# The first channel product of the last batch: 15 products for 3x3 by 3x2 blocks in place of 11 of 12

## The chip, the cores and the metric

One core of a Trainium2 chip runs the whole program. The time is device microseconds of that core. The kernel before took 606.97 us, the median of three runs (605.12 to 607.92). Its profiled execution took 605.11 us, of which the profile's span covers 603.4 us.

## What is computed

A delta-rule recurrence (linear attention), followed by a mixer with a low-rank part and two channel products. Cut to what matters:

```python
# attention, batch 4, 8 heads, 768 tokens, 48 per head -> x of (4, 768, 384)
for t in range(S):
    y[:, :, t] = einsum('bhd,bhde->bhe', q[:, :, t], state)
    v_old = einsum('bhde,bhd->bhe', state, kt)
    state = state + bt * einsum('bhd,bhe->bhde', kt, vt - v_old)
# mixer, for every batch
h = xt @ U @ V                           # rank 32, over the tokens
u = x + h.transpose(0, 2, 1)             # (768, 384)
ch = maximum(u @ w_ch1, 0.0) @ w_ch2     # 384 -> 1536 -> 384
out = u + ch
```

The change concerns `u @ w_ch1` (and the cut at zero behind it) for the last of the four batches. There `w_ch1` is 3 blocks of 128 input channels by 12 blocks of 128 hidden channels (`f` is a hidden block), and `u`, turned so that channels lie on partitions, is 3 blocks of 128 channels by 768 tokens.

## The kernel before, in words

**Stages.** For each batch, `recur` runs the recurrence in 12 chunks of 64 tokens, with `norms`, `grams` and `blocks` preparing each half batch. `load_weights` (L742) reads the weights as 64-bit numbers and converts them in the first 120 us or so. The mixer of a batch goes in three groups of 256 tokens: `front(b, i)` adds the low-rank part (the adds are L1073) and turns the result (L1090, copied by L1093); `wide(b, i)` makes the first channel product (`channels`, L1142 and L204), the sums for the second (`add_up`, L1163, and `last_sum`, L1170) and the second product (`narrow`, L1230) as seven half-products of 128 by 192 in place of eight, whose results `gather` adds to X (L1176) and stores. The mixer of one batch overlaps the recurrence of the next.

**The last batch** has no recurrence to overlap. All its 768 tokens are turned into `ut_last` first, and its first channel product runs for all tokens at once in `quick(f)` (L848), for the six pairs of hidden blocks f and f+6. Such a pair is 2 x 3 blocks of weights by 3 x 2 blocks of tokens (two halves of 384 tokens), which would be 12 products of 128x128 by 384 columns. Two of the three channel blocks are handled by a scheme of seven products in place of eight (Strassen's, in Winograd's form), the third by four plain ones: 11 in all. It needs sums of weight blocks (`weight_sums`, L823: n1, s2, s4 for each f, and one in place, L836) and mixes of token blocks (`token_sums`, L839, five, L845). All products are issued by `mm` at L859. Running sums in PSUM are copied out by ACT (L877, L881, L886), added to by DVE (L868) and cut at zero by ACT (L863, or L927 straight from PSUM). The output `hs_last` lies in `slot0`, the turned tokens in `slot1`; both are free once the recurrence is over.

**PSUM.** Eight banks: four pairs, and two 'mix' banks (6 and 7) that overlap the last pair. A quick part takes a pair (px, pz) and one mix bank (py).

**The order of work** is written out in full: ORDER (L52) is a list of tokens, one for each step of one of some 660 parts. A part is a generator, numbered in the sequence in which parts are begun; its yields are steps on a named engine, or needs that must have been emitted before. `.2` on a token says which bank pair or mix bank the step takes, `q` that it goes in quarters of the array. Each engine works its steps in the order of this list; the semaphores between engines follow from the data.

Of the kernel before, what the change touches and what calls it, by code (L numbers as in the profile page):

```python
# [23 lines left out]
def kernel(ctx: ExitStack, tc: tile.TileContext, q: bass.AP, k: bass.AP, v: bass.AP, beta: bass.AP, moe_U: bass.AP, moe_V: bass.AP, moe_w_ch1: bass.AP, moe_w_ch2: bass.AP, out: bass.AP):  # L24
# [28 lines left out]
    1 0 1 0 1 0 1 0 37 1 21 22 21 22 21 2 14.0 21 22 36 22 176 38 2 176 15.1 39 36 39 38 178 177.2 37 36 178  # L53
    20 36 179.3 38 177 39 177 38 177 43 17.0 179 39 179 179 18.1 26 19 179 37 23 181 2 24 23 2.3 179 2 37 23
    182.1 2 123 2 12 2 179 32.3 24 12 180 26 182 183 24 184.0 19 24 177 12 19 43 177 29.3 184 177 19 186 19
    182 187.2 19 19 33.3 19 188 41 40 184 30.1 187 40 19 3.3 187 124 187 3 19 187 124 19 40 187 19 190 124 19
    191.0 3 23 3 122 19 192 124 187 19 122 191 19 19 191 191 122 191 19 125 191 191 196 196.2 35 194 197 194.1
    197 34 198 41 196 197 41 194 196 41 198 127 189.3 3 197 12 194 40 197 27 125 198 185.0 27 198 127 198 198
    194.2 27 122 189 199 122 197 122 194 34 126 196.1 42 194 34 196 34 25 194 34 126 194 25 34 193 194.2 185
    194 193 34 193 34 193 34 194 122 194.2 194 196 193 196 193 196 194 122 194 196.1 196 27 200 195 122 196  # L60
    195 5.2 122 128 195 34 42 195 185 5.1 128 201 195 122 34 196.0 5 34 196 189 195 5 34 196 4.2 34 196 34
    202.3 34 6.1 202 4 202 34 34 6.0 4.2 6 204 122 6 207.3 208 204.1 4 129 208 206 208 206.0 129 208 122 208
    4.2 122 209 204 209 4 210 206 122 208 206 4.2 209 207 122 209 211.0 209 122 204 207 4 209 4.1 212 204.2 4
    204 122 207 206.1 204 130 204 206 204 130 122 203 4.3 122 213 214.2 211 206 206 211 206 204.1 203 4 122
    211 4.3 203 204 4 131 203 206.0 205 203 131 206 203 205 4.3 204 122 206 204.1 122 205 216 4 122 205 204
    214 205 132 206.0 214 205 206 132 204 52 215.3 204 206 4.1 122 206 4 122 217 218.0 4.1 215 122 214 215
    141.2 215 4 133 133 218 141 122 137 4.1 122 218 7.2 54 218 4 219 54 7.0 53 122 54 142 7 142 53 7 142 53
    142 142 122 134 142 122 134 143 142 53 143 220 143 53 4.1 221.2 4 8.0 122 4.1 143 4 135 143 135 143 54 144
    143 144 54 56 144 122 53 144 122 8.1 53 54 144 8 144 54 222 145 145 145 122 8 145 144 136 4.0 221 4 223.1
    136 221 4.0 46 221 56 145 4 54 122 145 53 122 224 146 4.2 223 4 225.0 223 122 4.2 223 146 145 4 49.1 226  # L70
    146 227 226 4.2 225 4 229.1 225 226 4.2 225 146 4 146 226 4.0 229 4 230.2 229 122 4.0 229 146 4 231 122
    232.1 4.0 146 230 4 232 122 230 230 46.0 232 66 233 47.2 234 66 233 147 232 66 235 236.0 233 66 233 237.1
    236 66 67 236 152.2 66 67 237 236 236 237 66 67 237 51 237 67 152 67 50.0 67 147 55 152 44 67 147 238 69
    44 147 67 147 69 66 148.1 147 44 55 148 51 69 152.2 147 55 148 69 51 239.0 55 152 56 148.1 239 59 55 239
    51 56 62.2 148 51 51 149.0 247 51 63.2 51 149 249 148 68 149 250 68 59.2 51 148 68 51 150.0 253 68 51 252
    60.1 68 51 151.2 255 150 55 150 257 68 153.1 151 258 68 256.0 151 259 55 240 260 254.2 55 240 256 153 68
    243 254 254 254 240 254 51 153.1 241 228.2 241 153 241 243 261 51 51 51 51 244 51 265 265.1 65 256 265 262
    228 265 242 265.1 265 267 244 228 256 263 256 265 265 265 267.2 64 264 267 264 265.1 264 245 267 268 57
    264 44 154.0 57 265 265 245 269 264 57 264 154 57 154.2 270 265.1 265 64 270 265 267.0 267 154 64 246 267
    265 267 267 64 266 64 266 271 267.2 266 64 271 9.0 266 272q 64 9 64 272 64 9.1 272 283.0 272 64 283 283 9  # L80
    272 64 9.0 284 285.1 64 267 267 273 9 266 64 64 273 64 274 286 64 64 274 64 266 275 287 288 64 275 64 276
    289 64 288 276 64 64 277 290 288 64 277 64 64 279 291 64 64 292 279 292 64 64 292 64 9.2 248.0 293 9 294
    9.2 280 9 248 248 64 278 267.2 267 64 9.0 267 295 285 9 267 280 285 64 285 281 299 78 301 298 297 298 302
    296.0 298 299.2 298 301.1 299 301 300 298 281 300 299 301 300 300 282 303 303 300 300 298 304 301.2 301
    304 299.1 299 301 305q 301 299 9.2 305 9 9.2 305 299 305 9 9.2 305 9 316.1 317 9.2 296 9 306q 296 296 306
    9.2 306 9 306 9.0 306 9 318.2 319 316 9.0 307q 9 316 316 9.0 307 9 320.1 307 9.0 307 9 9.0 9 307 9.0 321
    320 9 318 320 322 9.0 318 322 79 308 320 9 318 79 322 79 308 79 79 80 324 9.1 251.0 79 80 9 323.2 79 80
    251 9.1 309 251 80 9 82 9.0 82 325.1 9 323 72 9.0 323 79 323 309 9 80 80 72.2 326 80 310 327 82 80 9.0
    328.2 82 9 9.0 328 325 9 325 328 9.0 325 328 310 9 328 73.1 330 331 75.0 332 331 333 329.2 331 334.1 9.0
    334 312q 9 334 334 9.0 77 334 329 312 329 329 336.1 312 312 9 70 70 9.2 312 9 70 77 9.0 76.2 9 77 339 81  # L90
    9.0 337 336 338 9 81 341.2 336 311 9.0 336 313q 9 77 77 77 9.1 313 9 77 342.0 77 313 9.1 313 9 77 9.1 77
    313 9 77 344 342 343 341 340.1 77 341 92 342 77 342 314 92 341 340 92 340 92 77 314 92 93 77 92 93 77 92
    93 77 155.0 93 345 93 77 93 93 335.2 155 346 93 155.1 77 346 92 81 77 315 95 155 85 81 335 81 95 155.0 335
    95 77 85.1 155 81 88.2 347 348 77 347 89.0 360 77 86.1 94 362 77 94 361.2 364 77 94 349q 361 77 94 349 361
    94 156.0 77 349 94 349 77 81 156 366.1 94 77 349 81 367 361 156.0 77 94 366 77 350 361 77 366 156 77 350
    366 77 366 351 368 370 91 351 372 369 90 371 352 369 373 371 352 70 83 371 353 375 83 371 369 374 353 369
    83 374 90 354 376 83 354 90 374 377 365.2 90 90 370.0 372.1 378 372 370 365 371 372 356 370 371 365 95 90
    90 378 356 378 90 379 369 90 372.1 370.0 380 369 372 370 90 372 357 370 90 372 90 370 90 357 381 90 382
    10.2 90 363.1 10 10.0 157.2 10 355 10.0 358 10 90 363 90 358 385 90 363 359 90 386 157 386 10.0 387 384.1
    138 10 157q.2 138 90 10.0 157 388 90 90 388 10 138 138 138 399 10.2 90 383.0 384 383 389q 10 383 138 138  # L100
    384 90 10.2 384 389 10 400.0 138 389 10.1 90 389 10 138 389 90 10.2 401 138 400 10 390q 400 138 90 400
    10.1 390 90 10 402.2 390 10.0 390 10 138 90 10.1 390 10 404 90 403.0 402 405 10.1 402 90 391 402 405 10
    138 90 391 90 90 392 406 405 392 408 104 407 10.2 138 407 393 10 411 410 138 409 138 138 407 412.1 138
    10.2 409 403 10 393 409 403 409 395 413 407 414 403 414 415 10.2 414 408.0 10 408 408 10.2 412 10 410.0
    412 410 106 408.2 412 408 410 106 395 408 408 106 106 106 105 396 394 106 105 416 407 105 106 105 396 417
    105 106 105 397 418 105 105 407 397 419 98 409 101.1 420 409 102.0 421 98.2 422 107 99.1 424 107 107 426
    10.0 427.2 10 420 10.1 107 427 428.0 107 387 427 427 108 398 428 107 10 428 427 428 107 103 428 107 410.1
    429.2 10.0 10 96 410 430 96 10.0 410 430 431q 108 410 10 108 431 96 103 442.1 108 431 10.0 431 10 103 10.0
    103 10 429 103 431 429 103 10.0 429 442 443 10 444.2 103 10.0 103 10 432 442 103 442 103 10.0 423.1 10 103
    10.0 444 103 432 444 10 444 423 423 433 446 103 103 10.0 445.2 103 10 425.1 10.0 425 433 425 10 103 447  # L110
    10.1 445 10 434q 445 448 445 103 10.0 434 10 103 449.1 434 10.2 434 10 448 450.0 10.2 434 10 449 451 103
    10.2 449 103 435 449 10 103 450 103 435 450 119 450 103 119 448 436 452 119 103 119 96 436 119 118 119 121
    103 453 158.1 119 118 103 118 103 118 454 118 438q 103 103 119 438 158 118 454 118 158.2 454 438 103 118
    438 158 438 103 103 158q.0 456 111 455 103 114.1 158 103 115.2 457 111.0 462 120 112.1 120 464 437 439 121
    466 461 117 120 459 460 121 460 120 458 468 120 159.2 460 120 467.0 458 159 120 469.1 467 120 467 439 469
    467 460 469 469 467 116 469 440 458 470 109 458 109 440 471 109 116 441 472 116 472 116 116 116 159q.2 116
# [1197 lines left out]
```

## Time and profile before

| | before |
|---|---|
| median of three runs | 606.97 us (605.12 to 607.92) |
| the profiled execution | 605.11 us, span 603.4 us |
| PE busy | 560.4 us, 93% |
| DVE busy | 391.5 us, 65% |
| ACT busy | 244.1 us, 40% |
| mean granted TensorE clock | 0.955 |
| the rewritten stage (L859) | 515.2 to 557.7 us, 66 products |

PE is matrix products, DVE and ACT the two vector engines that read PSUM and make the sums. A product of fp32 operands leaves two records (two passes), so 66 products are 132 records. "Granted clock" is the share of full speed that TensorE was given. A group's line gives the source line, engine, operation, what is written and read, shapes and count, then busy time and mean duration in ns, then the engine's idle time just before those instructions and what ended it.

### The profile page before, as it was taken

The numbers are of one execution on the slowest core, as the hardware profiler recorded it, in microseconds if no ns is written. First come the engines' busy times: TensorE is split into PE (matmuls) and PEld (weight loads), VectorE is DVE, ScalarE is ACT, GpSimd is POOL, SyncE is SP. The second block draws the span as 40 slices with busy tenths as digits, with TensorE's granted clock in tenths as the row PEclk, the third lists the DMA queues.
The fourth block names the chain that finished last, engine by engine and source line by source line (L and its number), as shares of the span: only waits on it lengthen the run. The fifth ranks groups of instructions, "written<-read, shape, count | busy, mean of one in ns | idle before, by whom it ended". The sixth has DMA issues, their size and how long they took to land. (4 is left out here: it accounts for less than half of the span.)

```text
span 603.4 us, 24671 instructions
## 1 busy us (share of the span) xinstructions
PE 560.4 (93%) x11133; PEld 471.2 (78%) x11133; DVE 391.5 (65%) x979; ACT 244.1 (40%) x520; POOL 98.0 (16%) x169
## 2 busy tenths in 40 slices
PE   5566799999999999999999999999999999999997
PEld 4465778678788788789879877989889769656997
DVE  4899755899896229999983699898413226132542
ACT  2776974652314444263243532622532231344000
POOL 8420140630101032321004203210010000000000
PEclk9957569998999999999999999999999999999999
DMA  9963487730000061520004405200000000000000
GB/s 140 169 165 90 126 204 187 118 74 3 30 0 17 17 101 42 112 52 7 16 3 80 101 5 86 64 20 4 29 2 3 30 2 1 27 1 0 27 27 26
DMA packets 63850, 33.34 MB, mean 55 GB/s; under 512 B 50817, under 2 KB 61825, under 8 KB 63745
## 3 DMA queue, kind: packets, MB, share of 16 engines
q1 hardware_dynamic: 56800, 23.21, 17.6%
q0 software_dynamic: 5344, 8.27, 6.8%
q8 instruction: 87, 1.43, 1.0%
q10 hardware_dynamic: 1600, 0.30, 0.3%
q14 instruction: 19, 0.15, 0.1%
HBM read 27.03 MB, written 4.72 MB: 53 GB/s over the span
## 5 line engine op out<-in xcount | busy, mean ns | idle before, releaser
L1142 PE MATMUL P<-ut,w_sb 128*128 128x256 f32 x384 | 88.7, 384 | 0.3 <-ACT hs L1112 0.2
L1142 PEld LDWEIGHTS P<-ut,w_sb 128*128 128x128 f32 x384 | 71.1, 190 | 11.9 <-issue 1.8
L1230 PE MATMUL P<-w_sb,hs 128*128 128x192 f32 x456 | 79.5, 329 | 0.2 <-DVE X L1176 0.2
L1230 PEld LDWEIGHTS P<-w_sb,hs 128*128 128x128 f32 x456 | 73.9, 190 | 2.0 <-DVE X L1176 0.6
L463 DVE TENSOR_TENSOR xt<-xt,prod 128x112 f32<-128x112 f32 (+21 forms) x200 | 64.6, 323 | 6.9
L462 DVE TENSOR_TENSOR prod<-gs,xt 128x112 f32<-128x112 f32 (+21 forms) x200 | 63.7, 318 | 3.7
L1176 DVE TENSOR_TENSOR X<-X,P 128x192 f32<-128x192 f32 x85 | 29.4, 349 | 49.2 <-PE P L1230 45.8
L1112 ACT ACTIVATE hs<-P 128x512 f32<-128x512 f32 x48 | 28.7, 597 | 72.0 <-PE P L1142 53.7
L204 PE MATMUL P<-ut,w_sb 64*64 64x256 f32 x768 | 52.6, 384 | 1.7 <-ACT hs L1112 1.1
L1230 PE MATMUL P<-w_sb,S 128*128 128x192 f32 x240 | 43.3, 337 | 0.7 <-DVE X L1176 0.7
L1230 PEld LDWEIGHTS P<-w_sb,S 128*128 128x128 f32 x240 | 40.3, 195 | 1.6 <-DVE X L1176 1.4
L714 DVE TENSOR_TENSOR s<-s,P 128x192 f32<-128x192 f32 x40 | 14.0, 350 | 41.9 <-PE P L708 34.4
L304 POOL DMA_DIRECT2D slot<-in_k_dram x44 | 29.4, 674 | 64.5 <-PE P L708 46.9
L605 ACT COPY X<-P 64x192 f32<-64x192 f32 x96 | 30.0, 312 | 21.3 <-PE P L622 19.8
L581 ACT COPY slot<-zz 32x384 f32<-32x384 f32 x64 | 32.5, 509 | 6.9 <-DVE zz L467 3.5
L401 PE MATMUL P<-slot 48*64 48x64 f32 x1536 | 30.8, 232 | 4.6 <-ACT slot L389 4.4
L401 PEld LDWEIGHTS P<-slot 48*64 48x64 f32 x1536 | 28.0, 146 | 8.6 <-ACT slot L389 5.7
L585 POOL MEMSET slot<- 32x384 f32 x32 | 13.3, 421 | 129.7 <-PE P L556 113.5
L378 PE MATMUL P<-ident,slot 128*128 128x128 f32 x192 | 27.2, 294 | 6.8 <-DMA slot<-in_k_dram 6.8
L859 PE MATMUL P<-slot,w_sb 128*128 128x384 f32 x96 | 32.9, 486 | 0.0
L204 PEld LDWEIGHTS P<-ut,w_sb 64*64 64x64 f32 x768 | 25.1, 133 | 9.2 <-ACT hs L1112 1.8
L1230 PE MATMUL P<-w_sb,slot 128*128 128x192 f32 x180 | 30.4, 327 | 0.9 <-DVE X L1176 0.9
(176 smaller groups left out, 993.5 us busy)
## 6 DMA issues: line engine op xcount, KB each, us to landing
X<-in_moe_w_ch_dram SPq DMA_DIRECT2D x12, 384.0 KB, 4.4
out_dram<-X SPq DMA_DIRECT2D x22, 192.0 KB, 1.9
wide<-in_moe_w_ch_dram SPq DMA_DIRECT2D x10, 384.0 KB, 4.3
slot<-in_k_dram SPq DMA_DIRECT2D x48, 72.0 KB, 4.3
slot<-in_k_dram POOLq DMA_DIRECT2D x44, 72.0 KB, 4.5
slot<-in_q_dram POOLq DMA_DIRECT2D x32, 72.0 KB, 4.6
slot<-in_q_dram SPq DMA_DIRECT2D x32, 72.0 KB, 5.2
slot<-in_v_dram SPq DMA_DIRECT2D x32, 72.0 KB, 3.1
```

Source lines behind the costliest of these rows:

```text
L204: nc.tensor.matmul(to[half(g)], w[half(r), half(g)], x[half(r)], start=start, stop=stop, skip_group_check=True)
L304: queue.dma_start(out=t[half(1 - g if name == 'z' else g), :, to, 0:D], in_=src[b, 4 * g + s, hf * UC * L:(hf + 1) * UC * L, :].rearrange( ...
L401: nc.tensor.matmul(p_g[half(g ^ par * i), par, c], kq[rows, c, j, 0, half(g)], kq[rows, c, j, i, half(g)], start=True, stop=True)
L462: nc.vector.tensor_tensor(out=prod, in0=gb[:, :, j:j + 1, j + 1:].to_broadcast([128, split, m, w]), in1=xb[:, :, 0:m, j:j + 1].to_broadcas ...
L463: nc.vector.tensor_tensor(out=xb[:, :, 0:m, j + 1:], in0=xb[:, :, 0:m, j + 1:], in1=prod, op=ALU.subtract)
L581: nc.scalar.copy(pg[quarter(i), :, at, :, a:a + BK], cut(zc, h)[quarter(i)].rearrange('p r (c j) t -> p r c j t', j=2))
L605: nc.scalar.copy(x[half(c % 2), c // 2, 4 * D * g:4 * D * (g + 1)].rearrange('p (j r d) -> p r j d', r=2, d=D), states(p_y)[half(g)])
L859: nc.tensor.matmul(to, w, t, start=start, stop=stop, skip_group_check=True)
L1112: nc.scalar.activation(hs[:, fs[0]:fs[1] + 1:fs[1] - fs[0]], p_f, ACTF.Relu)
L1142: nc.tensor.matmul(p_f[:, x], w(x, t), ut[:, t], start=t == 0, stop=t == KT - 1)
L1176: nc.vector.tensor_tensor(out=to, in0=to, in1=p, op=ALU.add)
L1230: nc.tensor.matmul(to, of[0], of[1], start=of[2], stop=of[3], skip_group_check=True)
```

## The change

The 12 hidden blocks are put in four sets of three, in the order in which they are stored (COLUMNS: 0, 1, 2, 6, 7, 8, 3, 4, 5, 9, 10, 11; set e is entries e, 4+e and 8+e). For one set, 3 x 3 blocks of weights by 3 x 2 blocks of tokens would be 18 products; a bilinear scheme makes them with 15 (the table FIFTEEN: bank, weight or mix of weights, tokens or mix of tokens, whether the product starts the bank afresh, the output block that is touched, and the sign). Four parts `quick(e)` replace six `quick(f)`, 60 products replace 66. A part holds three banks; of the 15 products, 10 add to the sum that the bank already holds, and after each product the bank is read once (`touch`): ACT copies it, or its negative, to an output block that is still empty, DVE adds it to or subtracts it from one that is not. After the last touch of a block ACT cuts it at zero. A product waits for the touch of the product that used its bank before.

The weight mixes are eight tiles of 128x512 (for all four sets at once), made by 14 operations of DVE: seven once the weights are there (`weight_sums`), seven among the front parts of the last batch (`late_sums`), when the room in `slot1` is free. They no longer overwrite w1. The token mixes are 12. w1 lies block by block (`[128, FT, KT, 128]`), so that one slice holds four hidden blocks of one input block; loads, conversions and the other products address the same data by the new layout. ORDER is written anew throughout.

```diff
-    w1_sb = const.tile([128, FT // 2, KT * 256], FP32, name='w1_sb')
+    w1_sb = const.tile([128, FT, KT, 128], FP32, name='w1_sb')
...
+    def mix_weights(steps):
+        for x, how, a, c in steps:
+            a, c = (third(*z) if isinstance(z, tuple) else w1_mixes[z] for z in (a, c))
+            yield op('dve')
+            nc.vector.tensor_tensor(out=w1_mixes[x], in0=a, in1=c, op=how)
...
+    def late_sums():
+        yield need(('front', LAST, 0))
...
+    FIFTEEN = ((0, '4', '4', True, (1, 1), -1), (1, (0, 1), '14', True, (0, 0), -1), (0, (1, 2), '3', False, (1, 0), -1), (2, (2, 2), '6', True, (2, 1), -1), (0, '1', (2, 0), False, (0, 0), 1), (1, '13', (1, 0), False, (1, 0), 1), (0, '15', '15', False, (0, 1), 1), (2, '9', '9', False, (0, 1), -1), (0, '5', (0, 1), False, (2, 1), 1), (1, '7', '7', False, (2, 0), -1), (0, (2, 0), '12', False, (2, 0), 1), (2, (1, 0), '2', True, (1, 0), 1), (1, (2, 1), '11', False, (2, 1), -1), (2, (0, 0), '8', True, (0, 0), 1), (1, '10', '10', False, (1, 1), 1))
+
+    def quick(e):
...
+        def touch(s, p, **more):
+            at, sign = FIFTEEN[s][4:6]
+            old = [x for x in range(s) if FIFTEEN[x][4] == at]
+            if not old and sign > 0:
+                yield op('act')
+                nc.scalar.copy(c(*at), p)
+            elif not old:
+                yield op('act')
+                nc.scalar.mul(c(*at), p, -1.0)
+            else:
+                yield need(('touched', e, old[-1]))
+                yield op('dve')
+                nc.vector.tensor_tensor(out=c(*at), in0=c(*at), in1=p, op=ALU.add if sign > 0 else ALU.subtract)
+            emitted(('touched', e, s))
+            if all((FIFTEEN[x][4] != at for x in range(s + 1, 15))):
+                begin(cut(*at))
+        banks = [None] * 3
+        for s, (x, a, t, fresh, _, _) in enumerate(FIFTEEN):
+            yield need(*[('touched', e, max([y for y in range(s) if FIFTEEN[y][0] == x], default=-1))] * (s > 2 and s != 3), *([('tokens', int(t))] if isinstance(t, str) else []))
...
+            nc.tensor.matmul(banks[x], w1_sb[:, 4 * a[0] + e, a[1]] if isinstance(a, tuple) else w1_mixes[a][:, e], tokens(*t) if isinstance(t, tuple) else u_mixes[t], start=fresh, stop=True, skip_group_check=True)
+            begin(touch(s, banks[x], **dict(give=[('mix', y)]) if s == 13 else {}))
...
-            return [('cut', k, m, f) for k in ks for m in ms for f in fs] if b == LAST else []
+            return [('cut', m, f + HF * k) for k in ks for m in ms for f in fs] if b == LAST else []
```

The end of the new ORDER, from the front parts of the last batch (162 to 164; 139 is `late_sums`, 140 `token_sums`, 547 to 550 the second product of the group before, 572 to 575 the four quick parts, 567 and 568 the sums for the second product, 577 its first part, and the numbers from 581 on are touches and cuts in the order in which they were begun):

```diff
...
+    557 11 555 543 558 555 543 558 555 543 558 559 162.0 544 162 162.1 544 162 162.2 560 545 162 139 163.0 139
+    545 163 139 163.1 561 139 547 163 562 562 562 139 164.2 563 139 547 164 164.0 546 548 564 164 139 548 565
+    140 140 549 566 140 140 140 549 569 140 140 140 550 572.1 571 570 571 140 574.2 581 570 140 572 582 140
+    572 583 140 574 584 572.0 574 586 573.0 572 588 587 573 589 573 590 573.1 591 585 572 592 572 593 572 594
+    572 595 572 596 572 598 597 573 599 601 573 600 572 602 573 603 573 604 605 573 606 608 572 607 572 609
+    572 610 613 573 612 615 574.0 611 573 614 616 575.1 617 619 573 618 573 620 622 573 621 624 573 623 626
+    574 625 628 575 627 574 574 630 574 631 574 632 634 574 633 574 635 574 636 638 574 637 640 574 639 642
+    575 641 629 575.1 643 644 574 645 575 646 648 575 647 575 649 575 650 575 651 653 575 652 575 654 575 655
+    575 656 659 575 658 657 577 661 568 660 568 663 568 575 662 567 577 664 567 666 567 578 665 576 578 667
...
```

## The prediction

> **What bounds the kernel now.** I read the page first, then the busy time by stretches, then the chain of waits, and last the groups and the order in time of the stage that the change rewrites. TensorE (PE) is busy for 93% of the span. The stretches show where it is not:
>
> ```profile
> core 0: us, PE busy (x) PEld busy (x) DVE busy (x) ACT busy (x) POOL busy (x), PEclk, DMA share, GB/s
> ...
> 80.00:85.00 5.00, 4.95 (x131) 4.40 (x131) 3.59 (x7) 3.67 (x8) 0.79 (x2) 0.50 0.61 187
> 140.00:145.00 5.00, 3.76 (x203) 3.37 (x202) 4.96 (x8) 0.32 (x1) 0.98 (x1) 0.96 0.01 3
> 145.00:150.00 5.00, 5.00 (x136) 4.52 (x135) 4.97 (x10) 3.30 (x7) 0.00 (x0) 0.70 0.01 3
> 530.00:540.00 10.00, 10.00 (x33) 5.89 (x32) 3.78 (x8) 4.01 (x9) 0.00 (x0) 1.00 0.00 1
> 540.00:550.00 10.00, 10.00 (x33) 5.89 (x32) 3.36 (x7) 4.92 (x12) 0.00 (x0) 1.00 0.00 0
> ```
>
> From 515 us to 557 us PE is full at clock 1.00 while DVE and ACT are under half busy: there the number of products is the time. Early on the granted clock is at half (0.50 at 80 us) while PE is already full; the rivals come back to that.
>
> The chain of waits says the same in order of time (start, length, what):
>
> ```profile
> 515.17 42.57 PE P L859 x132
> 557.74 13.66 PE P L1230 x84
> 571.43 0.37 DVE X L1176
> 571.84 13.93 PE P L1230 x84
> ```
>
> L859 is the first channel product of the last batch: 132 records, two to a product of 128x128 by 384 columns, so 66 products in 42.57 us, **0.645 us each**, without a gap. Behind it stands the second product (L1230), also PE. The last two lines give the price of a real wait: PE stops, DVE reads a bank (modelled length 0.35 us), PE goes on 0.45 us after it stopped.
>
> The groups by shape give the durations, and the order in time gives the delay from a product to its reader:
>
> ```profile
> L868 DVE TENSOR_TENSOR slot<-slot,P 128x384 f32<-128x384 f32 x18 | 9.4, 551 | 23.6 <-PE P L859 23.6
> L863 ACT ACTIVATE slot<-slot 128x384 f32<-128x384 f32 x18 | 8.9, 521 | 12.0 <-DVE slot L868 12.0
> L877 ACT COPY slot<-P 128x384 f32<-128x384 f32 x6 | 2.8, 476 | 7.4 <-PE P L859 7.4
> L845 DVE TENSOR_TENSOR slot<-slot 128x384 f32<-128x384 f32 x5 | 2.6, 553 | 1.2 <-ACT slot L1093 1.1
> L836 DVE TENSOR_TENSOR w_sb<-w_sb 128x128 f32<-128x128 f32 x6 | 1.5, 284 | 0.0
> ```
> ```profile
> 515.01 0.81 PE L859 MATMUL P<-slot,w_sb 128*128 128x384 f32 x2
> 515.65 0.81 PE L859 MATMUL P<-slot,wide 128*128 128x384 f32 x2
> 515.85 0.48 ACT L877 COPY slot<-P 128x384 f32<-128x384 f32 x1 [5.70 <-PE P L859]
> ```
>
> A product starts at 515.01, the next at 515.65, and the reader of the first bank at 515.85: 0.84 us after the product's start. From a reader's end to PE: 571.43 + 0.35 = 571.78, and PE starts at 571.84, 0.06 us.
>
> **The change, step by step.**
>
> 1. *Products.* 6 quick parts of 11 become 4 of 15: 66 to 60. The new ones have the same 384 columns and the same weights of 128x128, so 6 x 0.645 = **3.87 us less on PE**, in a stage where PE is the path.
>
> 2. *Waits on banks.* This is where part of it goes back. Each running sum stays in its PSUM bank: a product adds to its bank, a reader adds the bank to its block of the output (`touch`), and the next product may add to that bank only when the reader is done. A part has three banks. If PE starts a product every 0.645 us and the same bank comes again two products later, 1.29 us have passed. The reader needs 0.84 + 0.55 + 0.06 = 1.45 us on DVE and 0.84 + 0.48 + 0.06 = 1.38 us on ACT: PE is short by 0.16 and 0.09 us. Three products later (1.93 us) there is room. So I read the end of the new ORDER token by token. Parts 572 to 575 are the four quick parts, called e0 to e3 here, and each of their tokens is the next of the 15 products. Products 6, 8 and 10 share bank 0, and 11 and 13 bank 2. The same bank two PE products apart, read by ACT: steps 6 to 8 of all four parts. Read by DVE: steps 8 to 10 of e0, e2 and e3; 12 to 14 of e0; 11 to 13 of e1, e2 and e3; 4 to 6 of e3. (In e1, 12 to 14 follows right on 11 to 13, and the first wait covers it.) Everything else is three or more apart, and at those places neither DVE nor ACT has a queue that is late. That makes 8 x 0.16 + 4 x 0.09 = **1.64 us more**. In the trace of before this wait does not occur in L859 (idle 0.0), so the size is an estimate from the rows above. The bounds are 0 (if the modelled ends of the products are late by 0.16 us) and twice as much, 3.3 us. I take 1.64, because the delays are direct rows.
>
> 3. *DVE and ACT in the stage.* The 18 adds (L868) become 36, at 0.55 us 9.9 us more; ACT has 24 first touches and 24 cuts where it had 18 copies, 18 cuts and 6 direct cuts (L927), some 2.9 us more. DVE was busy 3.4 to 3.8 us in 10, ACT 4.0 to 4.9: both stay below 7 in 10, so PE hides them, other than the waits of step 2.
>
> 4. *Token mixes.* 5 become 12, 7 x 0.55 = 3.9 us more of DVE. In the new ORDER seven stand ahead of the first quick product and five behind its first tokens. Before, the last turned tokens were copied at 509.36 + 0.80 = 510.2 and the first product began at 515.0. In the new ORDER that copy comes earlier (the turning product stands ahead of five of the seven second products of 1.95 us, not of three). The first products need two mixes (1.1 us). Cost 0, below nothing impossible, since PE had no gap there. If the cover were gone it would be the length of the missing mix, 0.55.
>
> 5. *Weight sums.* 24 of 128x128 (18 at 0.28, 6 at 0.284, 6.8 us) become 14 of 128x512. No such row exists: 128x384 takes 0.55 and 128x768 0.95 us, so about 0.69, 9.7 us together. Seven stand in the middle of the run, where DVE has had 18 and where a delay is bounded by one operation. Seven (4.8 us) stand among the front parts of the last batch, at 495 to 510 us, where DVE is busy 5.3 in 10. They are queued ahead of the adds L1073, and the turning products (L1090) wait for these. For the second group I get the add done 0.2 us before PE asks, for the third 0 to 0.2 us after. Cost 0 to 0.4; I take **0.1**.
>
> 6. *The end of the stage.* Before, three of six parts let the sums of the second product (L1163) begin. Now a part holds scattered columns, and all six sums wait for the last part. The new ORDER puts the first half-product of L1230 (1.95 us) between products 13 and 14 of e3, and so covers the last cuts. Followed through DVE: six sums, two touches and a gather end the one that is needed about when PE gets to it, 0 to 0.3 us late; I take **0.1**.
>
> 7. *Layout of w1.* Same pieces, same KB, same words to convert; products read the same 128 columns. Only L1005 now reads its 256 columns in two pieces: 0, at most its 3.0 us again, at 60 to 120 us where PE has gaps.
>
> 8. *The rest of ORDER* is written anew too, mostly neighbours swapped among the first 500 us. I put it at 0 with the bounds of the rivals.
>
> Sum: -3.87 + 1.64 + 0.1 + 0.1 = **-2.03 us**. The profiled execution took 605.11 us (span 603.4 and 1.7 around it), which would become 603.1. It lies at the low end of the runs shown (605.12 to 607.92); on their median, 606.97, the sum gives **604.9 us**, -0.33%.
>
> **The rivals.**
>
> *The waits do not bite* (readers release PE earlier than modelled): -3.87 + 0.2, 603.3 us. For it: the ends of products are modelled. Against: the 0.45 us stops around one 0.35 us read are real idle time. 0.23.
>
> *The waits are twice as long*, since readers queue behind the cuts: -3.87 + 3.3 + 0.2, 606.6 us. Against: ACT's and DVE's queues followed above. 0.05.
>
> *The clock, early: slower.* At 140 to 145 us PE idles 1.24 us, and in the next 5 us the clock is 0.70: 3 us at half, with PE full, 1.5 us lost. From about 29 to 87 us the clock is mostly 0.50, and in the last 7 us of that PE is full. A rewritten early order (step 8) that spreads the gaps differently lets the half clock last longer. Each microsecond longer costs 0.5 where PE is full. From 4 us on the gain of 2.03 is gone and it is slower than before; at 10 us it is 604.9 + 5 = 609.9 us. 0.12, nearly half of it beyond 0.5%. The same the other way, the 3 us at 145 gone and a little of the earlier stretch: 604.9 - 2 = 602.9 us. 0.10.
>
> [...]
>
> *The stage's own waits throw the clock to half*, as a mechanism of this kernel: 12 waits of 0.09 to 0.16 in 40 us, and one stretch of 3 us at half costs 1.5 us; from four on the change is slower by over 0.5%, and a whole stage at half would be 604.9 + 38.7 = 643.6 us. Against: after 571 us PE stops 0.45 us in every 14 us, as large a share, at clock 1.00. 0.02.
>
> That the change does not do what it says is excluded by its text: 60 products are issued.
>
> **How the numbers follow.** Forecast 0.48, the rivals as given. A measurement of this kernel can tell about 0.5% (3.0 us) from no change. Faster by more than that (below 603.9): waits that do not bite 0.23 and a better clock 0.10, 0.33. Within: 0.48 + 0.05 + 0.07 of the longer half clock, 0.60. Slower: the rest of it 0.05 and 0.02, 0.07. The range of 602.2 to 607.8 holds the forecast with its bounds, the waits of both kinds, the better clock but its edge, and the smaller part of the worse one; some 0.15 is left out.
>
> **What would show it.** Step 1: 120 records of the new product line, 486 ns each. Step 2: idle time of PE in front of them, about 1.6 us in 12 pieces, named DVE (8) and ACT (4), and a stage of 40.4 us where 42.57 stood. Steps 4 and 5: no gap ahead of its first product. Step 6: a gap of under 0.3 us ahead of the second L1230 groups. Step 8: PEclk in slices 2 to 10 of the page. The prediction is wrong if the stage is gapless (39 us), or if the time up to 500 us moves by more than 2 us.

## The result: slower by 0.7%

| | before | after |
|---|---|---|
| median of 12 runs each | 606.36 us (604.21 to 608.12) | 610.03 us (607.82 to 615.46) |
| the profiled execution | 605.11 us, span 603.4 us | 610.66 us, span 609.0 us |
| PE busy | 560.4 us, 93% | 564.6 us, 93% |
| mean granted TensorE clock | 0.955 | 0.941 |
| first product of the rewritten stage | 515.17 us | 521.65 us |
| length of the stage | 42.57 us, 66 products | 41.6 us, 60 products |

The ratio is 1.0074, with a 95% interval of 1.0048 to 1.0099. Ratios leave out runs in a slow state, which are 713.39 us of `early_old` and 608.73 us of `joins_late` further down.

The stage that the change is about became shorter by 0.95 us (42.57 to 41.62). In the profiled execution it begins 6.5 us later. So 6.5 - 0.95 gives the 5.6 us by which the profiled span is longer, and the loss lies ahead of the stage, in work of which the change mainly rewrote the order. How much it is varies from execution to execution: a second profile of the kernel after (607.23 us, `after_again` below) has its first product at 518.22 us. By the medians the loss ahead of the stage is 610.03 - 606.36 + 0.95 = 4.6 us.

The chain of waits of the kernel after, where the stage stands (start, length, what; the line of the products is L894 now, of the second product L1198):

```profile
511.90 9.75 PE P L1198 x60
521.65 11.15 PE P L894 x34
532.81 6.26 PE P L894 x18
...
562.62 1.95 PE P L1198 x12
565.22 11.71 PE P L1198 x72
```

Where one line stood before (42.57 us, 132 records), the product line is now broken into pieces: the breaks are products that waited for their bank. From 521.65 to 562.62 are 40.97 us for 59 products, and the 60th lies between the two L1198 lines: 562.62 + 1.95 + 0.645 = 565.22. There is no gap ahead of the first product (511.90 + 9.75 = 521.65) nor at the end.

The stretches within the stage, and one early:

```profile
80.00:85.00 5.00, 3.26 (x138) 2.84 (x129) 2.50 (x6) 3.62 (x7) 0.00 (x0) 0.50 0.41 147
...
530.00:540.00 10.00, 10.00 (x30) 5.04 (x29) 6.09 (x11) 3.78 (x9) 0.00 (x0) 1.00 0.01 2
540.00:550.00 10.00, 10.00 (x30) 5.09 (x29) 5.47 (x10) 5.91 (x13) 0.00 (x0) 1.00 0.00 0
```

In the stage there are 30 records in 10 us where 33 stood. PE still reads as full, because a record of 486 ns overlaps the next, which starts 0.32 us after it, and so covers idle times of 0.09 to 0.16 us; the count of records shows them and the busy column does not. DVE and ACT stay under 6.1 in 10, and the clock is 1.00. At 80 us PE is busy 3.26 us of 5 where it was 4.95, at the same half clock: that is where to look.

The groups that answer the readers of before:

```profile
L879 DVE TENSOR_TENSOR slot<-slot,P 128x384 f32<-128x384 f32 x36 | 19.9, 554 | 19.3 <-PE P L894 18.3
L864 ACT ACTIVATE slot<-slot 128x384 f32<-128x384 f32 x24 | 12.2, 521 | 11.7 <-DVE slot L879 11.2
L875 ACT ACTIVATE slot<-P 128x384 f32<-128x384 f32 x20 | 9.3, 486 | 14.5 <-PE P L894 14.4
```

The counts and durations (554, 521 and 486 ns) are those that the prediction worked with.

### The profile page after: what moved, and what is told of

It is laid out like the page before. It is cut to its first block, busy times and chain, and to the rows that moved or that the text cites. A ratio compares the mean times of both kernels' runs of the same rounds, so it can differ in the third digit from the quotient of the medians.

```text
span 609.0 us, 24691 instructions
## 1 busy us (share of the span) xinstructions
PE 564.6 (93%) x11121; PEld 471.4 (77%) x11121; DVE 409.4 (67%) x994; ACT 248.0 (41%) x526; POOL 97.6 (16%) x169
## 4 chain that ended last, share of the span: by engine, by line
PE 64%; DVE 26%; ACT 5%; issue 3%; DMA 1%; SPq 1%; ACTq 0%; DVEq 0%
PE P L1198 20%; PE P L1110 8%; PE P L205 8%; PE P L894 7%; DVE prod L463 6%; DVE xt L464 6%; PE P L379 3%; PE P L940 2%; PE P L402 2%; DVE zz L468 2%; PE P L616 1%; PE P L709 1%; DVE S L1131 1%; DVE slot L421 1%; PE P L623 1%
## 5 line engine op out<-in xcount | busy, mean ns | idle before, releaser
L1110 PE MATMUL P<-ut,w_sb 128*128 128x256 f32 x384 | 90.7, 390 | 0.2 <-ACT hs L1080 0.2
L1198 PE MATMUL P<-w_sb,hs 128*128 128x192 f32 x456 | 79.4, 329 | 0.4 <-DVE X L1144 0.4
L1198 PEld LDWEIGHTS P<-w_sb,hs 128*128 128x128 f32 x456 | 73.8, 190 | 3.4 <-issue 1.8
L1198 PE MATMUL P<-w_sb,S 128*128 128x192 f32 x240 | 42.8, 336 | 0.8 <-DVE X L1144 0.8
L1198 PEld LDWEIGHTS P<-w_sb,S 128*128 128x128 f32 x240 | 40.2, 195 | 1.6 <-DVE X L1144 1.5
L879 DVE TENSOR_TENSOR slot<-slot,P 128x384 f32<-128x384 f32 x36 | 19.9, 554 | 19.3 <-PE P L894 18.3
L1198 PE MATMUL P<-w_sb,slot 128*128 128x192 f32 x180 | 30.6, 327 | 0.9 <-DVE X L1144 0.9
```

Source lines behind the costliest of these rows:

```text
L1110: nc.tensor.matmul(p_f[:, x], w(x, t), ut[:, t], start=t == 0, stop=t == KT - 1)
L1198: nc.tensor.matmul(to, of[0], of[1], start=of[2], stop=of[3], skip_group_check=True)
```

## The experiments

The theory after the result: the order of the first 500 us costs some 6 us, and the product scheme gains about 1. The rivals: the new layout of w1 costs it; or the seven wide weight sums do; or the early clock gate swings on its own.

**The order undone, the order alone, the layout alone.** `old_order` is the kernel after with the order of before up to the front parts of the last batch, the seven early wide weight sums where 18 small ones stood. `new_order` is the reverse: the products, the layout and the sums of before, in the order of after.

```diff
 ORDER = """
-    1 0 1 0 1 0 1 0 22 1 21 22 21 2 21 39 14.0 21 22 38 22 177 36 2 177 15.1 37 38 39 36 179 178.2 20 38 179
+    1 0 1 0 1 0 1 0 37 1 21 22 21 22 21 2 14.0 21 22 36 22 177 38 2 177 15.1 39 36 39 38 179 178.2 37 36 179 20 36
...
```

> The changed kernel (15 products, new layout, 14 wide weight sums), but every step up to the front parts of the last batch in the order of the kernel before, with the seven early weight sums where 18 stood. In the profiles the first quick product starts 6.5 us later than before, and the stage itself is 1.6 us shorter. Theory (the rewritten order of the first 500 us costs the time): the loss of 6.5 us is gone, the gain of 1.6 stays and the end costs 0.6 more; 606.4 - 1.0 = 605.4, first quick product at about 515. Rival (the new code itself, layout or weight sums, makes the first 500 us longer): 610, first quick product at 520 or later. Rival (a chance of the clock): about 605, but also with the new order.

Measured: 604.23 us (602.21 to 609.1), ratio 0.9971 (0.9943 to 0.9998). The first quick product begins at 513.72.

> The kernel before (11 of 12 products, its layout, its sums), but every step up to the front parts of the last batch in the order of the changed kernel. Theory (order): 6.5 us longer up to the first quick product, 606.4 + 6 = 612.5. Rival (the new code): 606.4. Rival (chance of the clock): 606.4 on the mean.

Measured: 611.64 us (608.76 to 615.18, 8 runs), ratio 1.0086 (1.0049 to 1.0123). The order alone makes the kernel slower, without any of the new products.

`layout` is the kernel before with w1 block by block and nothing else:

```diff
-    w1_sb = const.tile([128, FT // 2, KT * 256], FP32, name='w1_sb')
+    w1_sb = const.tile([128, FT, KT, 128], FP32, name='w1_sb')
...
-        return w1_sb[:, y, 256 * t + 128 * PAIRS[y].index(f):][:, 0:128]
+        return w1_sb[:, 2 * y + PAIRS[y].index(f), t]
```

> The kernel before with w1 laid out block by block and nothing else changed: same order, same sums, same products. Theory (order): 606.4, within 0.3%. Rival (the layout costs, by loads, conversions or strided reads of weights): up to 610.

Measured: 604.79 us, ratio 0.9987 (0.9957 to 1.0017). The layout costs nothing that can be measured. The wide sums are in `old_order` too, so neither rival holds.

**Which part of the order.** An order can be cut only where both versions have done the same steps; steps 243 and 450 (about 57 and 90 us) are such places. `early_old` is the kernel after with its first 450 steps in the old order:

```diff
-    1 0 1 0 1 0 1 0 22 1 21 22 21 2 21 39 14.0 21 22 38 22 177 36 2 177 15.1 37 38 39 36 179 178.2 20 38 179
+    1 0 1 0 1 0 1 0 37 1 21 22 21 22 21 2 14.0 21 22 36 22 177 38 2 177 15.1 39 36 39 38 179 178.2 37 36 179 20 36
...
```

> The changed kernel with only the first 450 steps (about the first 100 us, where the clock is at half) in the order of before. Before and after differ by 3.6 us at 118 us and by 6.5 at 515. Theory (order): the 3.6 us are back, 610.0 - 3.6 = 606.4, and 2.9 us are still lost later. If the later loss only follows from the early one: 604 to 605. If the early order is not the cause: 610.

Measured: 606.6 us (604.56 to 609.88), ratio 1.0004 (0.9974 to 1.0033). So some 3.4 us of the loss are made in the first 450 steps, and some 2.4 behind them (606.6 against the 604.23 of `old_order`).

`mid_new` and `first_new` are `old_order` with one stretch in the new order: steps 243 to 450, and the first 243.

```diff
-    5.1 128 202 196 122 34 197.0 5 34 197 190 196 5 34 197 4.2 34 197 34 203.3 34 6.1 203 4 203 34 34 6.0 4.2 6
+    5.1 128 196 190 196 34 197.0 34 5 197 34 5 122 197 4.3 34 197 34 203.2 202 34 6.1 34 34 203 203 6.0 205 6 122
...
```

> The changed products with the old order everywhere (the run old_order, 604.2 us), but steps 243 to 450 of the list, about 55 to 90 us, in the changed kernel's order. There the new order puts all four joins of the second half batch (L519, L533 of the kernel before) ahead of the second chunk of the recurrence; the old one puts that chunk first. Theory (this interleaving delays the chain of chunks, and the first ready-made channel products L972 start 4 us later): 604.2 + 4 = 608. Rival (it is the first 243 steps, which shift the clock): 604.2.

Measured: 607.99 us (605.21 to 612.2), ratio 1.0038 (1.0007 to 1.0068), 3.8 us over `old_order`. As the theory had it.

```diff
-    1 0 1 0 1 0 1 0 37 1 21 22 21 22 21 2 14.0 21 22 36 22 177 38 2 177 15.1 39 36 39 38 179 178.2 37 36 179 20 36
+    1 0 1 0 1 0 1 0 22 1 21 22 21 2 21 39 14.0 21 22 38 22 177 36 2 177 15.1 37 38 39 36 179 178.2 20 38 179 36 37
...
```

> The run old_order with only the first 243 steps (about 55 us) in the changed kernel's order. Theory: 604.2. Rival (the first steps shift the clock): 606 to 608.

Measured: 606.62 us (603.59 to 610.67), ratio 1.0014 (0.9979 to 1.0048): between the theory and its rival, and the interval holds both. This is inconclusive by itself; the next pair speaks to it.

`mid_old` is the test from the other side: the kernel after with steps 243 to 450 in the old order (the edit of `mid_new` the other way round), and the kernel after once more on the same chip.

> The changed kernel with steps 243 to 450 of the order (about 57 to 90 us) put back as they stood before; all else as changed. If the interleaving of the joins with the recurrence of batch 0 in that stretch is the main part of what step 8 lost (3.8 us when that stretch alone was made new in the old order), the time is 606.2 us, 3.8 below the changed kernel's 610.0. Rival: the loss is made in the first 243 steps, and this stretch only passes it on: 609 to 610 us.

> The changed kernel unaltered, as the base for the run before it on the same chip: 610 us, both theories.

Measured: `mid_old` 606.54 us (605.35 to 611.11), ratio 1.0023 (0.9999 to 1.0046), and `after_again` 610.34 us, ratio 1.0068 (1.0038 to 1.0097). By the medians this stretch costs 3.8 us from both sides. The ratios to the kernel before, which take out the difference between sets of runs, give 4.1 us (1.0038 against 0.9971) and 2.7 us (1.0068 against 1.0023), so the size is known to about 1 us. `mid_old` and `early_old` differ by the first 243 steps alone, and by 0.06 us (1.2 by the ratios).

**What happens in that stretch.** There the last joins of half batch 1 (`joins`, L520 to L569 of the kernel after: groups of 24 or 48 products of 64x16 and 32x32) go on PE among the chunks of batch 0's recurrence (L616, L623, L692, L709), and the first ready-made channel products (L940; L972 before) follow. They begin at 86.51 us before, 86.05 in `mid_old`, but 90.13 after. (By itself that start proves little: in `first_new`, whose profiled execution took 610.27 us where its median is 606.62, they begin at 90.32 with the old stretch.) The waits of PE from 57 to 93 us, in the kernel after (line, what it waited for: us in total, times, longest):

```profile
PE P L520 <- DVE zz L468: 2.6, 1, 2.6
PE P L569 <- issue: 2.1, 1, 2.1
PE P L534 <- ACT S L488: 1.5, 2, 1.2
PE P L557 <- issue: 1.1, 1, 1.1
```

and in `mid_old`, where no line names "issue":

```profile
PE P L706 <- DVE z L696: 1.2, 2, 0.8
PE P L706 <- ACT zz L521: 0.9, 1, 0.9
PE P L706 <- ACT slot L570: 0.9, 1, 0.9
```

"Issue" is time in which PE waited for nothing that the profile shows. In the kernel after two such stops are on the chain itself:

```profile
68.85 1.46 PE P L534 x44
73.21 1.14 issue
77.68 2.05 issue
82.97 0.68 PE P L616 x16
```

The first falls into the middle of one join group: one product of 32x32 at 72.98 us, its neighbour of the same group at 74.36. Both belong to one step of ORDER, and the kernel has nothing between them for which PE could wait. PE's waits from 57 to 93 us, each row from one profiled execution:

| kernel | steps 243 to 450 | PE busy | "issue" | all other waits |
|---|---|---|---|---|
| before | old | 29.98 us | 0.7 us | 5.7 us |
| `old_order` | old | 30.71 | 0 | 5.2 |
| `early_old` | old | 30.23 | 0.2 | 5.5 |
| `mid_old` | old | 29.95 | 0 | 6.0 |
| `first_new` | old | 28.36 | 0.5 | 6.9 |
| after | new | 27.20 | 3.5 | 5.5 |
| `after_again` | new | 27.38 | 2.2 | 6.3 |
| `mid_new` | new | 26.83 | 3.2 | 5.6 |
| `new_order` | new | 26.11 | 4.0 | 5.6 |

The waits for other engines are much the same in both kinds. What the new order adds is the stops without a releaser: 2.2 to 4.0 us where steps 243 to 450 are new, against 0 to 1.6 in the twelve runs that start from the old stretch (the 1.6 is `spaced`, below). By the means, 3.2 and 0.5, they are some 2.7 of the 3.8 us. What ends them is told in the last section.

**One delay in the stretch, and its tail.** Three versions ask which swap makes the stops. They start from `spaced`, told below, which has the old order up to the fronts. In `chunk_late` six steps of the recurrence (part 4) go behind the joins' first products, as in the new order:

```diff
-    5.1 128 202 196 122 34 197.0 5 34 197 190 196 5 34 197 4.2 34 197 34 203.3 34 6.1 203 4 203 34 34 6.0 4.2 6
-    205 122 6 208.3 209 205.1 4 129 209 207 209 207.0 129 209 122 209 4.2 122 210 205 210 4 211 207 122 209 207
+    5.1 128 202 196 122 34 197.0 5 34 197 190 196 5 34 197 4.2 34 197 34 203.3 34 6.1 203 203 34 34 6.0 6 205 122
+    6 208 205.1 129 208 207 208 207.0 129 208 122 208 122 209 205 209 210 207 4 4.2 211.3 4 4.2 4 122 208 207 4.2
...
```

> The version with alternating quick parts and the old order (601.7 us), with one thing moved: six steps of batch 0's recurrence (its second chunk: the copy of the state, two products on PE and two sums on DVE, and the output product between them) go behind the joins' first products of half batch 1, on PE and on DVE, as the new order has them. Nothing else is moved. If this one delay is what the stretch lost, the time is 603.5 to 605.5 us (2 to 4 more). Rival: the stretch lost by its many small swaps together, and this one is taken up before the first ready-made channel product: under 1 us more, 601.7 to 602.6 us.

> The version with alternating quick parts and the old order once more, as the base for the run before it on the same chip: 601.7 us, both theories.

Measured: `chunk_late` 602.27 us (600.05 to 603.18, 6 runs), ratio 0.9925 (0.9897 to 0.9954), and its base `spaced_again` 602.96 us, ratio 0.9962 (0.9931 to 0.9992). The delay is there and costs nothing: the second chunk's sum comes at 64.04 us where its base has 61.80, but the fourth at 72.73 against 72.16, and the ready-made products at 85.57 against 85.97. No "issue" line stands among its waits. The rival holds, and the theory of the one late chunk falls.

`joins_late` and `joins_late2` put steps 319 to 384 alone, the joins' last groups, into the new sequence:

```diff
-    4.2 210 208 122 210 212.0 210 122 205 208 4 210 4.1 213 205.2 4 205 122 208 207.1 205 130 205 207 205 130 122
+    4.2 210 208 122 210 212.0 210 122 205 208 4 210 4.1 213 205.2 4 205 122 208 207.1 205 205 205 130 207 204 130
...
```

> The version with alternating quick parts and the old order (601.7 and 603.0 us in two sets), with the steps 319 to 384 alone put in the sequence of the new order: the recurrence's chunks 5 and 6 ahead, and behind them the last four join groups of half batch 1 on PE, one behind the other, each waiting for ACT and DVE. If the stops of PE in that tail are what the stretch of 57 to 90 us lost, PE's first ready-made channel product comes 3 to 4 us later than the 85.6 to 86.0 us it has without the move, and the time is 605 to 606.5 us. Rival: here too the slack behind takes it up, as it did for the second chunk: the ready-made product within 1 us of 86, and 601.7 to 603 us; then the loss needs the swaps of both places together.

> As the version with the tail of the joins moved, but with the PSUM bank pairs given out so that each group's bank is read before it is written again (there, one group of half batch 1 lost its sums that way). Steps 319 to 384 in the sequence of the new order, all else the old order with alternating quick parts. If the tail is what the stretch lost: the first ready-made channel product 3 to 4 us after 86.0, and 605 to 606.5 us. Rival, which the run before it already leans to: within 1 us of 86 and 601.7 to 603 us.

In both, all instructions run but a bank pair is written again before its last read: in the first one group of joins of half batch 1 is lost, in the second, as far as the order tells, a half of the output of chunk 3 of batch 0. Measured: 602.5 us, ratio 0.9958 (0.9931 to 0.9986), and 602.15 us, ratio 0.9931 (0.9904 to 0.9959); ready-made products at 85.08 and 86.27 us, no "issue" stop in this stretch. So the tail by itself seems to cost nothing either. This is weaker than `chunk_late`: a read that is lost can take a wait with it.

`joins_back` puts the same steps of the kernel after back into the old sequence, and leaves the joins' middle groups (steps 243 to 319) as changed. The lines are broken at other places; the tokens differ from the 319th on, behind 207.2:

```diff
...
-    4.1 205 122 209 207.2 205 130 207 4 204 130 122 205.0 207 214 4.1 122 207 204 4 215.2 207 204 4.1 122 213
+    4 209 122 4.1 209 209 211 122 209 205 4 211 211 213.3 212 205 4.1 205 122 209 207.2 4 130 207 205 130 122 204
...
```

> The other way round: the changed kernel (610.0 and 610.3 us in two sets) with steps 319 to 384 alone put back in the old sequence. If the tail is what was lost, 606.5 us, as with the whole stretch put back, and the first ready-made channel product at 86 to 87 us in place of 90.1. If the loss needs both places, the second chunk's delay ahead of it and the tail, undoing one is enough to take most of it away: 606.5 to 608 us. If it lies in neither, 609 to 610 us.

Measured: 608.46 us (607.08 to 612.63), ratio 1.0046 (1.0016 to 1.0076); ready-made products at 88.71 us, "issue" 3.4 us. About half of the loss goes, 1.9 of 3.8 us, though the interval overlaps that of the kernel after. The stops stay, so the new sequence of the tail is not needed for them. What they need lies within steps 243 to 319; the late chunk alone (`chunk_late`) does not make them, and which other swap does is not settled.

**The waits on banks.** Two versions of `old_order` change only in which turn the 60 products come. In `spaced` two quick parts take turns, product by product, so that a bank comes again after six products or four, never two. In `serial` the parts go one after the other.

```diff
-    164.1 546 548 564 164 139 548 565 140 140 549 566 140 140 140 549 569 140 140 140 550 572.2 571 570 571 140
-    574.0 581 570 140 572 582 140 572 583 140 574 584 572.0 574 586 573.1 572 588 587 573 589 573 590 573.1 591
+    164.1 546 548 564 164 139 548 565 140 140 549 566 140 140 140 549 569 140 140 140 550 572.2 571 570 573.1 571
+    140 581 572 570 140 582 573 140 140 583 572 584 573 585 572.0 586 573.1 587 572 588 573 589 572 590 573 591
...
```

> The run old_order with the 60 products reordered: two quick parts alternate product by product, so that the same bank comes four products later at the earliest. Theory (PE waits for the touch wherever the bank comes again two products later, 2.9 us in all in the traces): the stage is 38.7 us of products without a wait, 604.2 - 2.9 = 601.3. Rival (something else than the banks stretches the products, such as contention with DVE and ACT reads): 604.2, and products still 0.69 us each.

Measured: 601.68 us (600.66 to 606.19), ratio 0.9936 (0.9908 to 0.9963), and 602.96 in the second set above: faster than both kernels. Its chain has the stage in one piece again, 60 x 0.645 = 38.70:

```profile
515.27 38.70 PE P L891 x120
553.97 13.66 PE P L1195 x84
```

```diff
-    574.0 581 570 140 572 582 140 572 583 140 574 584 572.0 574 586 573.1 572 588 587 573 589 573 590 573.1 591
+    140 581 572 570 140 582 572.0 140 140 583 572 584 572 585 572 586 572 587 572 588 572 590 589 572 591 572 592
...
```

> The run old_order with the quick parts one after the other, no interleaving: 24 places where the bank comes again two products later, in place of 13. If a wait costs only its own length (0.09 on ACT, 0.16 on DVE): 2.9 us in all where that pricing gives 1.8 for old_order, 605.3. If each wait costs 0.10 more, since the next weights are not loaded ahead while PE waits: 5.5 us where old_order has 2.9, 606.8.

Measured: 609.8 us (605.67 to 613.54), ratio 1.0069 (1.0038 to 1.01). The stage takes 45.44 us, 6.74 over 38.70: more than both theories gave. That is 3.8 of the 5.6 us by which it is slower than `old_order`; in the profile the stage also begins 1.9 us later (515.64 against 513.72), which nothing here explains. The order in time of `old_order` shows the price of one wait. L891 is the product, L876 DVE's touch, L869 ACT's:

```profile
522.59 0.81 PE L891 MATMUL P<-slot,power 128*128 128x384 f32 x2
522.79 0.48 ACT L869 COPY slot<-P 128x384 f32<-128x384 f32 x1 [0.68 <-PE P L891]
523.32 1.56 PE L891 MATMUL P<-slot 128*128 128x384 f32 x4
...
524.27 0.56 DVE L876 TENSOR_TENSOR slot<-slot,P 128x384 f32<-128x384 f32 x1 [0.21 <-PE P L891]
524.88 0.30 PEld L891 LDWEIGHTS P<-slot,w_sb 128*128 128x128 f32 x2 [0.62 <-DVE slot L876]
```

The product behind ACT's read starts 523.32 - 522.59 = 0.73 us after the one ahead of it, 0.085 late. Two products then stand in 524.88 - 523.32 = 1.56 us where 1.29 would do: 0.27, of which 0.16 is the wait on DVE. The other 0.104 is the first product's own. After a wait, one record of 590 ns stands among those of 486 ns (L891: 486, 486 and 590 ns at least, median and most, in `old_order`; 486 throughout in `spaced`). The kernel after has 12 such records and 12 waits, 8 on DVE and 4 on ACT, as many as step 2 of the prediction counted (the expectation of `serial` says 13). From start to start they are 8 x 0.164 + 4 x 0.086 = 1.66 us, and 12 x 0.104 = 1.25 us come on top: 2.91 of the 2.92 us that its 41.62 us stand over 38.70.

`serial` has 24 such records, 2.5 us, and 24 waits. Of these 21 are of 0.09 to 0.17 us, 2.9 us together. The other three, 0.45 us each, are at the changes of part, where ACT's first read of the next part is queued behind a cut that waits for DVE. The chain at the first of them:

```profile
526.82 0.56 DVE slot L876
...
527.40 0.52 ACT slot L861
527.93 0.39 ACT slot L872
...
528.36 3.05 PE P L891 x8
```

PE's next product waits for L872 (ACT's touch), this for L861 (the cut), this for L876.

## Why the prediction failed, step by step

*Step 8, the rest of ORDER,* "I put it at 0 with the bounds of the rivals", is the step that failed. It costs some 5 to 6 us: 610.03 - 604.23 = 5.8, or 6.1 with the second set, and 4.6 by the medians of before and after. What the term left out are in the main stops of PE without a releaser, each of which ends 1.2 to 1.8 us after a block of instructions landed (last section): 3.2 against 0.5 us from 57 to 93 us. The prediction's own sign for this came: the time up to 500 us moved by more than 2 us. Of the loss, 3.8 lie in steps 243 to 450 (shown from both sides), about 2.4 behind step 450, and the first 243 steps have nothing (`mid_old` against `early_old`) or up to 2.4 (`first_new`); that is not settled. "Mostly neighbours swapped" was no argument for 0: a swap also moves work against the transfers that run beside it (behind the two blocks of the last section, the transfer of the next sets out 2.3 to 3.4 us after PE has entered, with the old stretch 0.3 to 1.1 us). Where the 2.4 lie is settled only in part: from 250 to 372 us PE waits 2.8 to 3.1 us for other engines in the six traces with the new order there and 1.8 to 2.2 in the eleven with the old.

*The rival of the early clock* named 609.9 us, close to what came, and its sign: the half clock lasts longer, until 90.1 us and not 86.6, with 0.68 on the mean of the first 100 us and not 0.74. The rows of the page, before and after:

```profile
PEclk9957569998999999999999999999999999999999
PEclk9756559998999999999999999989999999999999
```

That the number is close is luck, for its mechanism is not what the runs show. In four other profiles the clock of the first 100 us is the same, 0.71 on the mean, and the new stretch is slower all the same: `old_order` took 602.72 us, `early_old` 605.26, `mid_old` 605.51 and `after_again`, the kernel after, 607.23. The half clock ends when the dense ready-made products begin: before, at 86.6 us, where they begin at 86.51, and after, at 90.1 us, where they begin at 90.13. That gaps of PE set the clock, as the rival had it, is not shown: in the kernel before, PE is busy 3.06 us from 55 to 60 us at a clock of 0.93, and 4.95 us from 80 to 85 us at 0.50.

The lower slice in the middle (0.66 at 400 to 405 us) is missing in the second profile of the same kernel, 1.00 there, so it is of one execution.

*Step 1* was right: 60 products, 0.645 us each (38.70 in `spaced`), 3.87 us less.

*Step 2* had the mechanism, the places and the length of the 12 waits (1.64 us predicted, 1.66 measured). It left out the 0.104 us by which the product after each of them is longer, 1.25 us, so that the whole is 2.92 us, inside the bound of 3.3. The stage lasts 41.6 us, not 40.4. The rival that the waits do not bite falls. So does the one of the clock at half: with 12 waits, and with 24 of 0.09 to 0.45 us in `serial`, the stage's clock is 1.00.

*Steps 3 to 7* were right: DVE and ACT under 6.1 in 10 us, no gap ahead of the first product or at the end, the layout at 0 (ratio 0.9987). (The 5.3 in 10 of step 5 is DVE's share from 500 to 510 us; from 495 to 510 it was 4.5, which favours the step.) Without step 8 the sum would be -3.87 + 2.92 = -0.95; `old_order` measured -1.7 (ratio 0.9943 to 0.9998).

## What to carry to other kernels

When a change rewrites an order written out in full, what stands far from its purpose can have a price too (here some 5 to 6 us): cut the two orders where both have done the same steps and compare stretch by stretch before putting it at nothing. A wait of PE on a bank cost here its own 0.09 or 0.16 us and 0.104 us in the product behind it; read it from start to start, and let two independent chains take turns so that it does not arise (in `spaced`, 60 products in 38.70 us without a wait). Where an engine stops and nothing releases it, look for a transfer of its instructions just ahead of the stop's end (here it landed 1.2 to 1.8 us before), and count whether the stops stand a whole number of blocks apart (here 256 and 257 records).

## What the runs showed of the hardware that was not expected

**PE stopped where a block of its instructions ended.** The stops without a releaser end soon after a transfer of a block of instructions. The trace lists these transfers (queue q8, 16384 bytes each). In the kernel after, from 71 to 73 us and from 72.9 to 74.3 us, the DMA queues show:

```profile
q8 instruction: 1, 0.02, 3.5%
```
```profile
DMA packets 0, 0.00 MB, mean 0 GB/s; under 512 B 0, under 2 KB 0, under 8 KB 0
```

One block, from 71.7 to 72.8 us, and then no transfer at all while PE stands until 74.36. Start to finish of these transfers, by the trace, and the ends of PE's stops:

| kernel | block landed | stop ended | difference | length of stop |
|---|---|---|---|---|
| after | 72.84, 78.31, 83.36 | 74.36, 79.73, 84.59 | 1.52, 1.42, 1.23 | 1.14, 2.05, 0.35 |
| `mid_new` | 76.25, 82.04 | 77.64, 83.28 | 1.39, 1.24 | 0.95, 2.32 |
| `after_again` | 74.77, 79.39, 84.03 | 76.11, 80.66, 85.52 | 1.34, 1.27, 1.49 | 0.66, 1.22, 0.35 |
| `new_order` | 75.81, 80.89, 85.87, 91.02 | 77.28, 82.11, 87.24, 92.34 | 1.47, 1.22, 1.37, 1.32 | 1.25, 1.50, 0.62, 0.61 |
| `joins_back` | 73.18, 78.36 | 74.64, 79.74 | 1.46, 1.38 | 1.11, 2.25 |
| before | 56.87 | 58.20 | 1.33 | 0.68 |

In the 17 traces PE stops 52 times without a releaser, for 0.19 to 2.32 us, and each stop ends 1.2 to 1.8 us after a block landed. (One of them stands at 392 to 403 us in every trace, that of the kernel before included; after, it is at 400.21 us, just ahead of the lower slice.) In the kernel after, a transfer takes 0.88 to 1.67 us, and from the start of the four that stand ahead of a stop's end to that end 2.2 to 2.6 us go by (71.74 to 74.36, for one).

The places of the stops agree too. In the kernel after, 87 blocks carry the 22,358 records of PE, products, weight loads and a few semaphore instructions: 257 to a block. Ahead of the ends of the three stops in the table stand 3009, 3265 and 3522 records, 256 and 257 apart. Counted in 256s, all 52 stops fall on place 193 or 194, and only 2 of the 830 other waits of PE fall within two places of there. These places fit a PE that stands where one block ends and the next has not come.

That its products are small and close together is not what sets the new order apart. The blocks that PE enters at 69.20 and 74.36 us in the kernel after last it 3.7 and 3.0 us; in the twelve runs that start from the old stretch, the same two blocks by count last 3.9 to 4.0 and 3.1 to 3.3 us. But the transfer of the next block begins 2.3 to 3.4 us after PE has entered in the four runs with the new stretch and in `joins_back`, and 0.3 to 1.1 us after in those twelve. One difference is what the DMA queues carry just then. In the kernel after, a load of weights keeps them at 0.91 from 69.2 to 71.7 us, and the block begins at 71.74. In `old_order` they are at 0.00 from 67.6 to 68.6 us, and the block begins at 69.00, 0.39 us after PE has entered. It fits that the new order brings weight loads and blocks together; no run moved a weight load alone.

That the missing block is what PE waits for is read from the times and places above; no run changed the fetch itself.

**A wait on a bank is longer than itself.** The two records of a product of fp32 operands start 0.32 us apart, but behind a wait the first takes 590 ns and not 486, and the second starts 0.43 us after it, 0.104 us more. In the kernel after, the load of a record's weights starts 0.32 us ahead of it in 105 of the 108 records that are not behind a wait (530.20 and 530.52, for one), and together with it, to 0.002 us, in the 12 that are (531.25 and 531.25). It fits that the lost lead makes the 0.104; no run shows the one without the other.
